# The fourth half's attention is woven in later inside the third half's feed-forward stage

## The chip, the cores and the metric

The kernel runs on one core of one Trainium2 chip. The metric is the time of one execution on the device in microseconds (us), lower is better. It is written directly against the engines: TensorE (PE) multiplies matrices into PSUM, VectorE (DVE) and ScalarE (ACT) read PSUM and write back to SBUF, GpSimd (POOL) copies and casts and issues DMAs, SyncE (SP) issues DMAs. Each engine works through its own queue in the order in which the program issued its instructions; engines meet only through semaphores.

## The reference

Windowed attention followed by a gated feed-forward network. `q`, `k`, `v` are (4, 8, 768, 64): 4 batches, 8 heads, 768 positions, head size 64.

```
scores = q @ k.T / sqrt(64) + bias          # bias = -slope[h] * distance
keep   = (key < 8) | (0 <= query - key < 96)
a      = softmax(scores where keep)         # per query
x      = (a @ v)  -> (3072 tokens, 512)     # heads side by side
out    = (relu(x @ w_gate) * (x @ w_val)) @ w_out    # d_ff = 1536
```

The output is 3072 x 512 in float32.

## The kernel before

**Halves.** The work is cut into 8 halves of 384 queries (half a batch each, `NHALF = 8`, numbered 0 to 7). Each half goes through attention, which yields `xT` (features in 4 chunks of 128, by 384 tokens), and then through the feed-forward network (FFN). The FFN of half `c` is a stage, and the attention of half `c + 1` is interleaved into that stage, piece by piece. Halves 0 and 1 have a start of their own; from half 2 on, all stages have one form. The change concerns the stage of `c = 2`, the third half, into which the attention of half 3, the fourth, is woven.

**Attention pieces** (`attention_pieces(s)`, 26 in all, for 4 pairs of heads p). `QKp.0` issues the pair's score matmuls (`pair_scores`, L397: 10 for odd halves, 8 for even ones, into 4 PSUM banks `x_ps`) and two exponentials on ACT (L406); `QKp.1` two more exponentials and the masks of the first group on DVE (L359, three for odd halves); `QKp.2` the masks of the second group (two). `AVp.0` and `AVp.1` (L427, five matmuls each) multiply by the values into one `x_ps` bank each; ACT takes the logarithm of the row sums (`lnd`, L436) and, after the second, the exponential of its negative (`rcp`, L441). `Np` (`piece_norm`, L446, two DVE products) writes the pair's chunk of `xT`. Two pieces are empty gaps. No attention piece issues a DMA.

**FFN pieces** (`ffn_pieces(c)`). `gate(fc)` does four matmuls (L518, one for each chunk of `xT`) into a bank `ff_ps`, and ACT's relu (L525) into `grelu`. `val(fc)` does the same with the other weights, and DVE multiplies by `grelu` into `ht` (L531). There are 12 pairs of gate and val. Behind some vals DVE adds columns of `ht` (`sum_de`, `sum_cb`, `sum_ad`, L567 to L576). Then come one output block of four parts (L538) and seven products `p4 p3 p1 p2 p5 p6 p7` (L583), whose results ACT and DVE collect and SP stores.

**The start of a stage.** The last chunk of `xT[c]` (chunk 3, from N3 of the stage before) comes late, so a stage begins with `begin`: the matmuls of gate 0 and val 0 on chunks 0 to 2, and for `c = 2` those of gate 1 as well. The piece `g0` is then only the matmul on chunk 3 plus the relu; likewise `v0`, and for `c = 2` also `g1`.

**Banks.** PSUM holds 3 `ff_ps` banks and 5 `x_ps` banks, each handed out in rotation. In the order g0, v0, g1, v1, g2, ... a bank comes round after three: val 1 needs the bank that gate 0's relu empties, gate 2 the one that DVE's product of val 0 empties, and in general val n+1 waits for relu n and gate n+2 for `ht` n. The scores, AVs and the products p2 and p5 take `x_ps` banks: scores 0 takes banks 0 to 3, scores 1 takes 4, 0, 1, 2, AV0 takes 3 and 4, scores 2 takes 0 to 3 (so its last bank is the one that N0 has to empty), and so on.

**The order.** Each engine's queue follows the program. `weave` issues the FFN pieces in order, each with a weight; a placed piece is issued as soon as its position, as a share of the total weight, has been passed. `spread(items, first, last)` places n items evenly from `first` to `last`.

```
def spread(items, first, last):
    n = len(items)
    return [(first + (i + 0.5) / n * (last - first), f) for i, (_, f) in enumerate(items)]

def weave(f_items, *placed):
    ...
    for t, f in f_items:
        f()
        done += t
        while ai < len(a_items) and a_items[ai][0] * total <= done:
            a_items[ai][1]()
            ai += 1
```

For `c = 2` the weights are 1.5 for `begin`, 0.15 for each of g0, v0 and g1, and 0.65 for every other piece (the three sums at the end weigh nothing): 22.75 in total. The loop is

```
    for c in range(2, NHALF):
        placed = []
        if c + 1 < NHALF:
            placed.append(spread(attention_pieces(c + 1), *((0.02, 0.8) if c == 2 else (0.0, 0.8))))
        if c + 2 < NHALF:
            load_qk(c + 2, 0, H)
            load_v_half(c + 2)
            placed.append(spread(early_pieces(c + 2), 0.25, 0.75))
        f1, f2 = ffn_pieces(c)
        weave(f1 + f2, *placed)
```

`load_qk` (SP) and `load_v_half` (POOL) fetch the half after the next; `early_pieces` are its casts (POOL), transposes (SP's DMA queue) and key copies (POOL for every half but 2).

Of the kernel before, what the change touches and what calls it, by code (L numbers as in the profile page):

```python
# [15 lines left out]
def kernel(  # L16
# [90 lines left out]
    def load_qk(s, h0, h1):  # L107
        b, half = divmod(s, 2)
        if s not in qs_of:
            qs_of[s] = late["stage"].tile([128, H, NN * D], FP32, name="qs")  # L110
            ks_of[s] = late["stage"].tile([128, H, NN * D], FP32, name="ks")
        for src, dst in ((k, ks_of[s]), (q, qs_of[s])):
            nc.sync.dma_start(
                out=dst[:, h0:h1, :],
                in_=src[b, h0:h1, half * QH : (half + 1) * QH, :].rearrange(
                    "h (p n) d -> p h (n d)", n=NN))
# [28 lines left out]
    def load_v_half(s):  # L145
        b, half = divmod(s, 2)
        if half == 0:
            load_v_globals(b)
            if s != 2:
                spread_v_globals(b)  # L150
        for j in range(4) if half == 0 else range(4, NT):
            load_v(b, j)
# [224 lines left out]
    def early_pieces(s):  # L377
        out = [(0.0, lambda p=p, i=i: piece_cast(s, p, i)) for i in range(2) for p in range(HP)]
        out += [(0.0, lambda n=n: piece_x(s, n)) for n in range(NN)]
        out += [(0.0, lambda p=p: piece_order(s, p)) for p in range(HP)]  # L380
        return out
# [26 lines left out]
    def piece_qk(s, p, g):  # L408
        if g == 0:
            pair_scores(s, p)  # L410
        if g < 2:
            pair_exps(s, p, g)
        if g > 0:
            masks(s, p, g - 1, steps_later)

    def piece_av(s, p, e):
        b, half = divmod(s, 2)
        h = 2 * p + e
        vb = vbuf[b % 2]
        av = psum["x"].tile([128, 512], FP32, name="x_ps")  # L420
        av_of[s, p, e] = av
        av3 = av[:, 0:QH].rearrange("d (n p) -> d n p", n=NN)
        todo = [by[half, j] for g in steps_later[half] for j in g]
        for i, (j, a, w, m) in enumerate(todo):
            es, c = es_of[s, p, j]
            z0 = 2 * D * h + (D if e == 0 else 0)
            nc.tensor.matmul(av3[:, :, a : a + w],  # L427
                             lhsT=vb[:, j, z0 : z0 + 128],
                             rhs=es[:, e, c : c + NN * w].rearrange("k (n p) -> k n p", n=NN),
                             start=(i == 0), stop=(i == len(todo) - 1),  # L430
                             skip_group_check=True)
        o0, d0 = (0, 64) if e == 0 else (64, 0)
        if e == 0:
            av_of[s, p, "l"] = rc_pool.tile([128, QH], FP32, name="lnd")
        ln = av_of[s, p, "l"]
        nc.scalar.activation(ln[o0 : o0 + 64], av[d0 : d0 + 64, 0:QH], AF.Ln, bias=0.0, scale=1.0)  # L436
        if e == 1:
            if s not in xT_of:
                xT_of[s] = xt_pool.tile([128, N_DC, QH], BF16, name="xT")
            rc = av_of[s, p, "r"] = rc_pool.tile([128, QH], FP32, name="rcp")  # L440
            nc.scalar.activation(rc, ln, AF.Exp, bias=0.0, scale=-1.0)  # L441

    def piece_norm(s, p):
        for e in range(2):
            r = slice(64 * e, 64 * e + 64)
            nc.vector.tensor_tensor(xT_of[s][r, p, :], av_of[s, p, e][r, 0:QH], av_of[s, p, "r"][r],  # L446
                                    op=ALU.mult)
# [45 lines left out]
    def attention_pieces(s):  # L493
        QK = lambda p: [(0.15, lambda g=g: piece_qk(s, p, g)) for g in range(3)]
        AV = lambda p: [(0.29, lambda e=e: piece_av(s, p, e)) for e in range(2)]
        N = lambda p: [(0.0, lambda: piece_norm(s, p))]
        g = QK(3)
        a = AV(2)
        gap = [(0.0, lambda: None)]
        return (QK(0) + QK(1) + AV(0) + N(0) + gap + QK(2) + AV(1) + N(1) + gap  # L500
                + g[0:1] + a[0:1] + g[1:2] + a[1:2] + g[2:3] + N(2) + AV(3) + N(3))
# [157 lines left out]
# [6 lines that stand above are left out]
        total = sum(t for t, _ in f_items)  # L665
        a_items = sorted((x for p in placed for x in p), key=lambda x: x[0])
        done, ai = 0.0, 0
# [6 lines that stand above are left out]
        for _, f in a_items[ai:]:  # L674
            f()
# [158 lines left out]
    for c in range(2, NHALF):  # L834
        placed = []
        if c + 1 < NHALF:
            placed.append(spread(attention_pieces(c + 1), *((0.02, 0.8) if c == 2 else (0.0, 0.8))))
        if c + 2 < NHALF:
            load_qk(c + 2, 0, H)
            load_v_half(c + 2)  # L840
# [3 lines that stand above are left out]
# [35 lines left out]
```

## Time and profile before

| what | us |
|---|---|
| median of 3 runs | 242.94 (242.49 to 243.86) |
| the profiled execution | 242.59 |
| its span, first to last instruction | 240.8 |
| PE busy | 233.0 (97 per cent) |
| DVE busy | 172.4 (72 per cent) |
| ACT busy | 153.4 (64 per cent) |
| POOL busy | 86.8 (36 per cent) |
| mean granted TensorE clock | 1.000 |

Times in the profile run from the span's first instruction. A line of the timeline gives the start, the duration, the engine, the line of the kernel, the operation, what it writes and reads with shapes, and how often; in square brackets stands how long the engine had been idle before it and what released it. Consecutive like instructions are merged into one line. The duration of merged matmuls includes the drain of the last one, so that the next matmul's start can lie before that end; starts are what to compare on PE. The stage of `c = 2` runs from 76.71 (the first matmul of `begin`) to 105.81 (the first of the next stage's).

### The profile page before, as it was taken

To read this page: it belongs to the slowest core of one execution; us is meant where nothing else is said; L and a number is where in the kernel's file an instruction comes from. 1 tells how busy PE (TensorE), PEld (TensorE's weight loads), DVE (VectorE), ACT (ScalarE), POOL (GpSimd) and SP (SyncE) were. 2 spreads that over 40 slices of the span, in tenths; PEclk is the share of its full clock that TensorE was granted. 3 is DMA by queue.
4 is the path that set the end of the run, shared out by engine and by line. 5 is a ranking of instruction groups with operands and counts; after the bars stand their busy time and mean duration, and the time that the engine had idled before them with its cause. 6 is when DMAs were issued, how large, how long until landed. Compare 5 with 4: busy or idle time off the path is not lost.

```text
span 240.8 us, 5354 instructions
## 1 busy us (share of the span) xinstructions
PE 233.0 (97%) x1937; PEld 146.3 (61%) x1945; DVE 172.4 (72%) x456; ACT 153.4 (64%) x347; POOL 86.8 (36%) x202
## 2 busy tenths in 40 slices
PE   7899999999999799999999999999999999999994
PEld 3655556665458456676658566676658566676663
DVE  7875965769577597866787679766888677764643
ACT  5897873438775777738864677738874677734330
POOL 6776893208514853603365041721514000000000
PEclk9999999999999999999999999999999999999999
DMA  6999999994976995748429945199251200030003
GB/s 203 187 197 177 258 233 219 180 153 81 268 159 158 295 148 109 48 136 261 89 46 110 256 131 108 25 174 268 44 95 44 87 3 0 3 123 9 4 24 107
DMA packets 69603, 31.42 MB, mean 130 GB/s; under 512 B 47160, under 2 KB 66616, under 8 KB 69576
## 3 DMA queue, kind: packets, MB, share of 16 engines
q0 software_dynamic: 31744, 8.71, 35.2%
q1 hardware_dynamic: 36616, 21.45, 34.7%
q10 hardware_dynamic: 1216, 0.92, 1.2%
q8 instruction: 15, 0.25, 0.4%
q14 instruction: 12, 0.10, 0.1%
HBM read 28.41 MB, written 6.29 MB: 144 GB/s over the span
## 4 chain that ended last, share of the span: by engine, by line
PE 92%; ACT 3%; DVE 3%; issue 1%; DVEq 0%
PE ff_ps L518 52%; PE ff_ps L538 10%; PE ff_ps L583 10%; PE x_ps L427 6%; PE x_ps L397 4%; PE x_ps L583 4%; PE t_ps L459 2%; PE s_ps L341 1%; PE t_ps L682 1%; PE t_ps L310 1%; PE t_ps L272 1%; ACT ef L347 1%; ACT es L406 1%; DVE es L359 1%; DVE xT L446 0%
## 5 line engine op out<-in xcount | busy, mean ns | idle before, releaser
L518 PE MATMUL ff_ps<-xT,wv 128*128 128x384 bf16 x384 | 80.2, 326 | 1.3 <-ACT grelu L525 1.2
L518 PE MATMUL ff_ps<-xT,wg 128*128 128x384 bf16 x384 | 80.7, 326 | 0.7 <-ACT grelu L525 0.4
L531 DVE TENSOR_TENSOR ht<-ff_ps,grelu 128x384 bf16<-128x384 f32 x96 | 53.0, 554 | 28.7 <-PE ff_ps L518 15.1
L525 ACT ACTIVATE grelu<-ff_ps 128x384 bf16<-128x384 f32 x96 | 47.2, 493 | 37.2 <-PE ff_ps L518 18.7
L518 PEld LDWEIGHTS <-wv 128*128 128x128 bf16 x384 | 36.1, 97 | 24.2 <-issue 2.5
L518 PEld LDWEIGHTS <-wg 128*128 128x128 bf16 x384 | 35.9, 98 | 24.5 <-issue 1.3
L406 ACT ACTIVATE es<-x_ps 128x360 bf16<-128x360 f32 (+2 forms) x96 | 36.6, 443 | 20.1 <-PE x_ps L397 20.0
L359 DVE TENSOR_TENSOR es<-es,m_all 128x432 bf16<-128x432 bf16 (+4 forms) x108 | 30.5, 327 | 9.6 <-ACT es L406 9.2
L446 DVE TENSOR_TENSOR xT<-x_ps,rcp 64x384 bf16<-64x384 f32 x48 | 26.6, 554 | 8.9 <-ACT rcp L441 8.2
L436 ACT ACTIVATE lnd<-x_ps 64x384 f32<-64x384 f32 x48 | 23.3, 485 | 12.3 <-PE x_ps L427 11.6
L538 PE MATMUL ff_ps<-wo_sb,ht 128*128 128x512 bf16 x112 | 29.7, 379 | 0.4
L363 POOL CAST kqc<-ks 128x384 bf16<-128x384 f32 x24 | 11.5, 525 | 34.7 <-DMA ks<-in_k_dram 34.7
L137 POOL DMA_DIRECT2D vbuf<-in_v_dram x25 | 21.6, 875 | 1.7 <-DMA wv<-in_moe_w_val_dram 1.5
L427 PE MATMUL x_ps<-es,vbuf 128*128 128x216 bf16 (+4 forms) x216 | 21.5, 225 | 0.0
L427 PEld LDWEIGHTS <-vbuf 128*128 128x128 bf16 x216 | 15.8, 97 | 7.7
L538 PEld LDWEIGHTS <-ht 128*128 128x128 bf16 x120 | 10.9, 97 | 9.4
L263 POOL COPY kT<-kqT 128x240 bf16<-128x240 bf16 x16 | 6.8, 423 | 24.6 <-DMA kqT<-kqc 21.9
L363 POOL CAST kqc<-qs 128x384 bf16<-128x384 f32 x24 | 11.9, 535 | 8.0 <-DMA qs<-in_q_dram 8.0
L259 POOL COPY kT<-kqT 128x360 bf16<-128x360 bf16 x10 | 6.2, 616 | 19.5 <-DMA kqT<-kqc 19.5
L441 ACT ACTIVATE rcp<-lnd 128x384 f32<-128x384 f32 x24 | 12.6, 524 | 0.8
L347 ACT ACTIVATE ef<-s_ps 128x720 bf16<-128x720 f32 (+2 forms) x16 | 10.9, 711 | 2.0 <-PE s_ps L341 1.8
L397 PE MATMUL x_ps<-kqT,kT 64*128 64x216 bf16 (+4 forms) x216 | 11.6, 224 | 0.2
(115 smaller groups left out, 252.7 us busy)
## 6 DMA issues: line engine op xcount, KB each, us to landing
out_dram<-osb SPq DMA_DIRECT2D x22, 256.0 KB, 2.5
ks<-in_k_dram SPq DMA_DIRECT2D x6, 768.0 KB, 5.8
qs<-in_q_dram SPq DMA_DIRECT2D x6, 768.0 KB, 11.7
vbuf<-in_v_dram POOLq DMA_DIRECT2D x21, 120.0 KB, 7.9
wg<-in_moe_w_gate_dram POOLq DMA_DIRECT2D x3, 512.0 KB, 8.3
wv<-in_moe_w_val_dram POOLq DMA_DIRECT2D x3, 512.0 KB, 9.9
wo_sb<-in_moe_w_out_dram POOLq DMA_DIRECT2D x1, 1536.0 KB, 19.9
kq<-in_q_dram ACTq DMA_DIRECT2D x2, 192.0 KB, 4.2
```

The source lines that it names most:

```text
L137: nc.gpsimd.dma_start(out=v_dst(b, NG + r0, NG + r0 + n, j), in_=v[b, :, KT * j + r0 : KT * j + r0 + n, :].rearrange("h p d -> p h d"))
L359: nc.vector.tensor_mul(for_all, for_all, mk)
L363: nc.gpsimd.tensor_copy(kqc[:, :, i].rearrange("t n (h d) -> t h n d", d=D)[:, 2 * p : 2 * p + 2], of[s][:, 2 * p : 2 * p + 2, :].rearrang ...
L406: nc.scalar.activation(es[:, e, 0:c], banks[e][:, 0:c], AF.Exp, bias=0.0, scale=scale)
L427: nc.tensor.matmul(av3[:, :, a : a + w], lhsT=vb[:, j, z0 : z0 + 128], rhs=es[:, e, c : c + NN * w].rearrange("k (n p) -> k n p", n=NN), s ...
L436: nc.scalar.activation(ln[o0 : o0 + 64], av[d0 : d0 + 64, 0:QH], AF.Ln, bias=0.0, scale=1.0)
L446: nc.vector.tensor_tensor(xT_of[s][r, p, :], av_of[s, p, e][r, 0:QH], av_of[s, p, "r"][r], op=ALU.mult)
L518: nc.tensor.matmul(st[key][:, 0:QH], lhsT=w_of(w, dc, fc), rhs=xT_of[c][:, dc, :], start=(dc == 0), stop=(dc == N_DC - 1))
L525: nc.scalar.activation(gr, psg[:, 0:QH], AF.Relu, bias=0.0, scale=1.0)
L531: nc.vector.tensor_tensor(ht[:, fc, :], psv[:, 0:QH], st["gr", fc], op=ALU.mult)
L538: nc.tensor.matmul(ps2, lhsT=ht[:, fc, n * 128 : (n + 1) * 128], rhs=wo_sb[:, fc, :], start=(fc == 0), stop=(fc == N_FC - 1))
L583: nc.tensor.matmul(st[key][:, 0:D2], lhsT=left(i), rhs=right(i), start=start and i == 0, stop=stop and i == N2 - 1, skip_group_check=not s ...
```

## The change

```
     for c in range(2, NHALF):
         placed = []
         if c + 1 < NHALF:
-            placed.append(spread(attention_pieces(c + 1), *((0.02, 0.8) if c == 2 else (0.0, 0.8))))
+            placed.append(spread(attention_pieces(c + 1), *((0.07, 0.82) if c == 2 else (0.0, 0.8))))
```

In the stage of `c = 2` alone, the 26 attention pieces of half 3 are placed from 7 to 82 per cent of the stage instead of 2 to 80. No instruction is added or removed; the order of issue changes. The other stages keep their order.

More of the change, by code (lines that the diff above doesn't have):

```diff
@@ L836 @@
         if c + 1 < NHALF:
-            placed.append(spread(attention_pieces(c + 1), *((0.02, 0.8) if c == 2 else (0.0, 0.8))))
+            placed.append(spread(attention_pieces(c + 1), *((0.07, 0.82) if c == 2 else (0.0, 0.8))))
         if c + 2 < NHALF:
```

## The prediction

> **What bounds the kernel now.** I read the chain that ended last first: 92 per cent of it is PE. PE works through one queue, so what the change can win is PE's idle time in the stage that it touches. Next I read busy time by stage, one window for each of the stages of c = 2, 3 and 4:
>
> ```profile
> core 0: us, PE busy (x) PEld busy (x) DVE busy (x) ACT busy (x) POOL busy (x), PEclk, DMA share, GB/s
> 76.70:105.80 29.10, 27.56 (x231) 17.84 (x231) 22.60 (x57) 18.90 (x44) 16.15 (x35) 1.00 0.91 141
> 105.80:132.70 26.90, 26.85 (x215) 17.45 (x215) 19.93 (x51) 18.34 (x44) 11.35 (x25) 1.00 0.70 134
> 132.70:160.20 27.50, 27.42 (x232) 17.86 (x232) 21.45 (x55) 18.98 (x44) 10.30 (x23) 1.00 0.62 129
> ```
>
> The stages of c = 2 and c = 4 have the same PE work (odd halves' attention in both, the same matmuls), yet c = 2 takes 29.10 us and c = 4 takes 27.50. The stage has 1.6 us that its twin does not need, at the same granted clock of 1.00. PE's timeline shows where:
>
> ```profile
> 77.69 0.65 PE L518 MATMUL ff_ps<-xT,wg 128*128 128x384 bf16 x3
> 78.27 0.48 PE L397 MATMUL x_ps<-kqT,kT 64*128 64x216 bf16 x10
> 78.68 0.34 PE L518 MATMUL ff_ps<-xT,wg 128*128 128x384 bf16 x1
> 78.86 0.33 PE L518 MATMUL ff_ps<-xT,wv 128*128 128x384 bf16 x1
> 79.02 0.33 PE L518 MATMUL ff_ps<-xT,wg 128*128 128x384 bf16 x1
> 80.58 0.81 PE L518 MATMUL ff_ps<-xT,wv 128*128 128x384 bf16 x4 [1.24 <-ACT grelu L525]
> 81.23 0.81 PE L518 MATMUL ff_ps<-xT,wg 128*128 128x384 bf16 x4
> ...
> 85.61 0.81 PE L518 MATMUL ff_ps<-xT,wv 128*128 128x384 bf16 x4
> 86.67 0.81 PE L518 MATMUL ff_ps<-xT,wg 128*128 128x384 bf16 x4 [0.25 <-DVE ht L531]
> ```
>
> A group of four FFN matmuls follows the next after 0.65 us (80.58 to 81.23), so one takes 0.163. The matmul at 79.02 frees PE at 79.18, and val 1 starts at 80.58: 1.40 us lost, waiting for gate 0's relu, since val 1 takes gate 0's bank. Val 4 at 85.61 frees PE at 86.26, and gate 5 starts at 86.67: 0.41 lost, waiting for DVE's product `ht` 3. ACT and DVE show why both came late:
>
> ```profile
> 78.63 1.52 ACT L406 ACTIVATE es<-x_ps 128x336 bf16<-128x336 f32 x4 [3.17 <-PE x_ps L397]
> 80.00 0.91 ACT L525 ACTIVATE grelu<-ff_ps 128x384 bf16<-128x384 f32 x2
> ```
>
> ```profile
> 77.26 1.13 DVE L446 TENSOR_TENSOR xT<-x_ps,rcp 64x384 bf16<-64x384 f32 x2
> ...
> 84.40 1.76 DVE L359 TENSOR_TENSOR es<-es,m_all 128x432 bf16<-128x432 bf16 x5
> 86.08 1.01 DVE L531 TENSOR_TENSOR ht<-ff_ps,grelu 128x384 bf16<-128x384 f32 x2
> ```
>
> ACT has four exponentials of scores 0 in front of relu 0, 78.63 to 80.15, though relu 0's matmul began at 78.68 and had drained by 79.02. DVE has both mask groups of pair 1, five masks in 1.76 us, in front of `ht` 3.
>
> **What the order becomes.** The weights sum to 22.75. Before, the pieces stand every 0.78/26 x 22.75 = 0.68, the first at (0.02 + 0.015) x 22.75 = 0.80; `begin` passes 1.5, so QK0.0 (0.80) and QK0.1 (1.48) follow it at once. After, they stand every 0.66, the first at (0.07 + 0.0144) x 22.75 = 1.92; `begin`, g0, v0 and g1 pass 1.5, 1.65, 1.8 and 1.95, so QK0.0 follows g1 and QK0.1 (2.58) follows v1 (2.6). Worked on in this way the orders are:
>
> before: begin QK0.0 QK0.1 g0 v0 g1 v1 QK0.2 g2 QK1.0 v2 QK1.1 g3 QK1.2 v3 AV0.0 g4 AV0.1 v4 N0 g5 v5 QK2.0 ... o0 N2 o1 AV3.0 o2 AV3.1 o3 N3 p4
>
> after: begin g0 v0 g1 QK0.0 v1 QK0.1 g2 QK0.2 v2 QK1.0 g3 QK1.1 v3 g4 QK1.2 v4 AV0.0 g5 AV0.1 v5 N0 g6 v6 QK2.0 ... o0 QK3.2 o1 N2 o2 AV3.0 o3 AV3.1 p4 N3
>
> So relus 0 and 1 are ahead of all exponentials, and only one mask group stands ahead of each `ht` (QK1.1 before `ht` 3, QK1.2 behind it). POOL's and SP's queues hold no attention instruction of this half, so their order is as before.
>
> **Cost, stall by stall.** (1) Val 1's wait. Chunk 3 of `xT` is ready when DVE ends at 77.26 + 1.13 = 78.39. `begin` ends at 76.71 + 9 x 0.163 = 78.18. Before, scores 0 filled that gap; now g0 waits for chunk 3. Relu 0 ended at about 80.50 and released val 1 at 80.58, so a release takes some 0.08: g0 starts at 78.47, a new stall of 0.29 (0.21 if the release is immediate, and not below that, since the norm's place on DVE does not move). Then v0 at 78.63, g1 at 78.80. Relu 0 starts when g0 has drained (0.33) at 78.84 and ends 0.49 later at 79.33, val 1 may start at 79.41. Scores 0 (0.09 of switch, seen as 81.88 to 81.97, and 0.41 of work) fill PE from 78.96 to 79.46. So val 1 starts at 79.46 without waiting: the 1.40 goes and 0.29 comes.
>
> (2) Gate 5's wait. From 79.46 on I laid the three queues side by side with the durations of the rows (relu 0.49, four exponentials 1.52, mask groups 0.65 and 0.60, `ht` 0.56, AV 0.31, `lnd` 0.49, `rcp` 0.52). `ht` 0 79.40 to 79.95, before gate 2 at 80.12; `ht` 1 to 80.88, before gate 3 at 81.93; the exponentials of pair 0 79.68 to 81.20, relu 2 81.15 to 81.64, before val 3 at 82.58; masks of pair 0 to 82.05, `ht` 2 to 82.55, before gate 4 at 83.23; masks QK1.1 to about 83.65, `ht` 3 to 84.20, before gate 5 at 84.84. Of the 0.41 nothing is left by this; if these masks go at the pace of the five (1.76 for what takes 1.25 elsewhere), `ht` 3 ends at 84.5, still in time.
>
> (3) What is late next. N0 now stands behind v5 and its sum: `ht` 5 from 86.65 to 87.21, the sum to 87.60, N0's first product to 88.17, release 88.25. It empties the bank that the eighth matmul of scores 2 takes. Scores 2 starts at 87.84, its eighth matmul at 88.13: a stall of 0.1. Before, N0's first product ended at 87.63 and scores 2 started at 88.07, no wait. The bounds are nothing (DVE 0.1 quicker) and 0.5 (DVE late by the 0.51 that the five masks lost); I take 0.1. `ht` 6 then ends at 89.30 for gate 8 at 89.66, `ht` 9, behind N1, at 94.45 for gate 11 at 95.0: covers of 0.36 and 0.5.
>
> (4) The end of the stage. AV3.1 moves behind o3, N3 behind p4, so `lnd` and `rcp` of pair 3 stand behind the block's copy on ACT; N3 ends about 102.3. Behind N3 on DVE stand the last sum, which p7 needs at 103.7, and p2's result at about 102.6. Chunk 3 is wanted by the next stage's g0 some 1.4 us after it starts near 104.4. Cost nothing; were N3 3 us later, the next stage would stall.
>
> The sum: the stage had stalls of 1.40 + 0.41 = 1.81; it now has 0.29 + 0.1 = 0.39, a gain of 1.42. Against the twin: 29.10 - 1.42 = 27.68, still 0.18 over c = 4, as the 0.29 and 0.1 against c = 4's own pauses lead one to expect. The later stages follow unchanged: their loads hang on their own stage's stores, and equal stages agree (c = 3 and c = 5 both 26.90, c = 4 and c = 6 both 27.50). The profiled execution was 242.59 and would be 241.2; the median of the three runs is 0.35 higher, which would give 241.5. I take 241.4 between them. With the bounds (0.21 at best; 0.29 + 0.5 + the whole 0.41 at worst) the gain lies between 1.6 and 0.6.
>
> **A rule against it.** The Trainium skill, in Perfetto Trace Analysis, section Matmuls, wants independent matmul groups to rotate through different PSUM banks, so that one's evacuation is overlapped by the next one's matmuls. By that rule alone the place of scores 0 before is right, for it is independent work in other banks exactly where PE waits for chunk 3, and taking it away would cost the 0.29 and make 242.9 of the profiled 242.59. The trace has the larger number on the other side: the same scores bring 1.52 us of exponentials in front of the relu that empties the bank.
>
> **The rivals.** *Half of it comes back* (no change that can be told): the norm's wait of 0.29 stays, gate 5's 0.41 stays because DVE falls behind once more, and scores 2 waits 0.3 for N0. The gain is 1.81 - 0.29 - 0.41 - 0.3 = 0.8, so 241.8 to 242.1. For it: DVE is the second busiest in this stage (22.60 of 29.10) and POOL's casts fall in the same stretch, where five masks took 1.76. Against it: `ht` 3 has 0.3 to 0.6 of cover. *The norms become the stall* (slower): N0, N1 and N2 each stand between PE and a bank of scores or an `ht` product, and each waits on ACT's `rcp`. If ACT's queue delays `rcp` and so each norm holds PE for over 0.47, three of them take the 1.42 back; at 0.9 each, 2.7, the kernel ends at 243.9. Against: N0 to N2 held PE not at all before (no such release on PE between 87 and 101), and each is moved by one FFN piece only. *The change does not do what it says*: the positions above leave no room for that, the margin (1.92 against 1.8 and 1.95 at g1) is arithmetic.
>
> **How the numbers follow.** 0.5 per cent, 1.2 us, is about what a measurement of this kernel can tell from no change. The forecast's centre of 1.42 lies just above it, so part of its own range (0.9 to 1.6) falls within. I give the forecast 0.72, the first rival 0.18, the second 0.10. Of the forecast's 0.72, some 0.60 lie beyond 0.5 per cent and 0.12 within, to which the first rival's 0.18 is added: faster 0.60, same 0.30, slower 0.10. The likeliest case's own range is 240.9 to 242.0. The range goes to 242.6 to take in the first rival and leaves out the second and a little at the low end.
>
> **What would show it.** In the changed profile, the stage from `begin` to the next `begin` should last 27.7 us. PE's timeline should show a gap of 0.3 released by DVE's `xT` ahead of g0 and none ahead of val 1; ACT should show two relus from about 78.8 and the exponentials behind them; gate 5 should follow val 4 and AV0.0 with no gap. The prediction is wrong if val 1 still waits for a relu, if PE shows new waits on DVE of over 0.5 us in total between 82 and 98, or if a later stage grows.

## The result and the profile after

The changed kernel takes 241.63 us (median of 6 runs, 241.15 to 242.14) against 242.94 us before: a ratio of 0.9939, 95 per cent interval 0.9917 to 0.9961, so 1.3 us or 0.6 per cent faster. Run again beside the experiments it took 241.75 us, ratio 0.9948 (0.9930 to 0.9965). The prediction was 241.4 us (range 240.9 to 242.6), with 0.6 on faster by over 0.5 per cent.

The busy time by stage, for the stages of c = 2 and c = 3 (the windows lie 0.1 to 0.2 us ahead of the stages' bounds, which are given below; us in the stretch, then the busy time of each engine with its instructions, the granted clock, the DMA share and GB/s):

```profile
core 0: us, PE busy (x) PEld busy (x) DVE busy (x) ACT busy (x) POOL busy (x), PEclk, DMA share, GB/s
76.70:104.50 27.80, 27.66 (x232) 17.99 (x231) 22.87 (x58) 18.88 (x44) 16.31 (x37) 1.00 0.92 146
104.50:131.40 26.90, 26.85 (x215) 17.45 (x214) 20.12 (x52) 18.34 (x44) 11.28 (x25) 1.00 0.71 134
```

From the first matmul of `begin` (76.89) to the next stage's (104.61) the stage now takes 27.72 us instead of 29.10, at the same clock. PE's timeline of the changed kernel, in the same columns as before:

```profile
77.87 1.06 PE L518 MATMUL ff_ps<-xT,wg 128*128 128x384 bf16 x4
78.77 0.32 PE L518 MATMUL ff_ps<-xT,wv 128*128 128x384 bf16 x1
78.93 0.33 PE L518 MATMUL ff_ps<-xT,wg 128*128 128x384 bf16 x1
79.19 0.48 PE L397 MATMUL x_ps<-kqT,kT 64*128 64x216 bf16 x10
79.60 0.82 PE L518 MATMUL ff_ps<-xT,wv 128*128 128x384 bf16 x4
80.26 0.81 PE L518 MATMUL ff_ps<-xT,wg 128*128 128x384 bf16 x4
...
84.02 0.81 PE L518 MATMUL ff_ps<-xT,wv 128*128 128x384 bf16 x4
84.67 0.47 PE L427 MATMUL x_ps<-es,vbuf 128*128 128x216 bf16 x5
84.98 0.81 PE L518 MATMUL ff_ps<-xT,wg 128*128 128x384 bf16 x4
...
87.98 0.67 PE L397 MATMUL x_ps<-kqT,kT 64*128 64x216 bf16 x10
88.58 0.82 PE L518 MATMUL ff_ps<-xT,wg 128*128 128x384 bf16 x4
```

Val 1 (79.60) follows scores 0 after their 0.41, gate 5 (84.98) follows AV0.0 after its 0.31: both waits are gone. Two short ones show: three matmuls of gate 1 and g0 are merged in the first line, and 1.06 where three in a row take 0.65 says that g0 stood apart; `begin` ends at 76.89 + 9 x 0.163 = 78.36, and v0 at 78.77 puts g0 at 78.61, so it waited 0.25. Scores 2 take 0.60 to the next start (87.98 to 88.58) instead of 0.41. On ACT the two relus are first:

```profile
78.96 0.87 ACT L525 ACTIVATE grelu<-ff_ps 128x384 bf16<-128x384 f32 x2 [3.33 <-PE ff_ps L518]
79.72 1.53 ACT L406 ACTIVATE es<-x_ps 128x336 bf16<-128x336 f32 x4
```

and on DVE `ht` 3 (83.64) stands between the two mask groups of pair 1, and N0 (87.72) behind `ht` 5 and its sum:

```profile
77.44 1.11 DVE L446 TENSOR_TENSOR xT<-x_ps,rcp 64x384 bf16<-64x384 f32 x2
...
82.92 0.64 DVE L359 TENSOR_TENSOR es<-es,m_all 128x432 bf16<-128x432 bf16 x3
83.64 0.56 DVE L531 TENSOR_TENSOR ht<-ff_ps,grelu 128x384 bf16<-128x384 f32 x1
84.17 1.26 DVE L359 TENSOR_TENSOR es<-es,m_all 128x384 bf16<-128x384 bf16 x2
...
87.72 1.14 DVE L446 TENSOR_TENSOR xT<-x_ps,rcp 64x384 bf16<-64x384 f32 x2
```

Of the 1.38 us that the stage won, the profiled execution (241.74 us, span 239.9) shows 0.9 at its end. The stage began 0.18 later than before, and the stages of c = 4 and c = 5 took 27.67 and 27.02 where they had taken 27.47 and 26.91: 0.31 of the gain was lost there.

### The profile page after: what moved, and what is told of

Its sections match the earlier page's. It is cut to its first block, busy times and chain, and to the rows that moved or that the text cites. A ratio compares the mean times of both kernels' runs of the same rounds, so it can differ in the third digit from the quotient of the medians.

```text
span 239.9 us, 5355 instructions
## 1 busy us (share of the span) xinstructions
PE 233.5 (97%) x1937; PEld 146.6 (61%) x1945; DVE 173.3 (72%) x456; ACT 153.4 (64%) x347; POOL 85.9 (36%) x202
## 4 chain that ended last, share of the span: by engine, by line
PE 91%; ACT 3%; DVE 2%; issue 1%; ACTq 0%
PE ff_ps L518 53%; PE ff_ps L538 9%; PE ff_ps L583 8%; PE x_ps L427 6%; PE x_ps L397 4%; PE x_ps L583 3%; PE t_ps L459 2%; PE s_ps L341 2%; PE t_ps L272 1%; PE t_ps L682 1%; ACT lnd L436 1%; PE t_ps L310 1%; DVE xT L446 1%; PE s_ps L321 1%; ACT rcp L441 0%
## 5 line engine op out<-in xcount | busy, mean ns | idle before, releaser
L359 DVE TENSOR_TENSOR es<-es,m_all 128x432 bf16<-128x432 bf16 (+4 forms) x108 | 31.2, 334 | 8.2 <-ACT es L406 7.8
```

The costliest lines, as they stand in the source:

```text
L359: nc.vector.tensor_mul(for_all, for_all, mk)
```

## The experiments

Two theories stood against each other. The queue theory is that of the prediction: the gain is the order on ACT ahead of relu 0 and on DVE ahead of `ht` 3. The rival: the attention as a whole lies later, and whatever crowding there was is eased. All results together; "stage" is the time from the first matmul of `begin` to that of the next stage in the one profiled execution of each kernel, "begin" where that first matmul lies. A ratio is taken against executions of the kernel before that were run beside that kernel.

| kernel | begin | stage | median us | ratio to before (95 per cent) |
|---|---|---|---|---|
| before | 76.71 | 29.10 | 242.94 | |
| the change | 76.89 | 27.72 | 241.63 | 0.9939 (0.9917 to 0.9961) |
| the change again | 76.81 | 27.72 | 241.75 | 0.9948 (0.9930 to 0.9965) |
| 1 exponentials first | 76.59 | 28.87 | 242.41 | 0.9976 (0.9962 to 0.9991) |
| 2 one mask group later | 77.26 | 29.11 | 242.39 | 0.9979 (0.9957 to 1.0001) |
| 3 scores first | 77.87 | 28.58 | 242.21 | 0.9972 (0.9955 to 0.9989) |
| 4 two exponentials ahead | 76.69 | 28.35 | 242.07 | 0.9963 (0.9946 to 0.9979) |
| 5 later still | 76.75 | 29.01 | 242.72 | 0.9992 (0.9977 to 1.0006) |
| 6 casts held back | 76.71 | 28.82 | 242.49 | 0.9976 (0.9959 to 0.9992) |
| 7 sum behind the norm | 76.22 | 27.53 | 240.76 | 0.9913 (0.9890 to 0.9936) |
| 8 both waits covered | 76.32 | 27.29 | 241.21 | 0.9925 (0.9898 to 0.9953) |
| 9 all even stages | 76.61 | 27.28 | 240.75 | 0.9912 (0.9888 to 0.9937) |
| 10 norm 3 sooner | 77.38 | 27.29 | 241.02 | 0.9923 (0.9905 to 0.9941) |

The column "begin" spreads over 1.65 us. The kernel before, the change and experiments 1 to 6 issue the same instructions in the same order up to `begin`, yet they range from 76.59 to 77.87; experiments 8 to 10, equal among themselves up to there, range from 76.32 to 77.38. So the stage tells the theories apart better than the time does; the change's stage came out at 27.72 both times.

**1. Exponentials first.** On the changed kernel, in the stage of c = 2, QK0.0 and QK0.1 go directly behind `begin`:

```
+               for i in range(2):
+                   items[i] = (0.05, items[i][1])
```

> The changed kernel, with one thing undone: QK0.0 and QK0.1 (the score matmuls of pair 0, its four exponentials and the masks behind them) stand directly behind begin again, as before; the other 24 attention pieces stay at their places of the change. Queue theory (the gain is ACT's order at the start, plus DVE's mask order ahead of ht 3): val 1 waits for relu 0 again, about 1.2 to 1.4 us on PE, no wait of gate 5; stage of c = 2 about 28.7 us, time about 0.4 us under before. Rival (the gain comes from the attention as a whole lying later, less crowding of DVE and ACT): 24 of 26 pieces lie where the change puts them, so nearly all of the gain stays, over 1.0 us under before.

Val 1 waits again, from 79.06 to 80.46:

```profile
80.46 0.81 PE L518 MATMUL ff_ps<-xT,wv 128*128 128x384 bf16 x4 [1.24 <-ACT grelu L525]
```

Gate 5 doesn't wait. The stage is 28.87, 0.17 over the expected 28.7: the expectation left out the wait of 0.19 in scores 2 (88.83 to 89.43, 0.60 as in the change). With 24 of 26 pieces where the change has them, 0.23 of the stage's 1.38 is left, and 0.24 of 0.6 per cent in the time. The rival, nearly all of the gain, falls.

**2. One mask group later.** On the kernel before, QK1.2 and AV0.0 change places:

```
+               items[5:7] = [(items[6][0], f) for _, f in (items[6], items[5])]
```

> The kernel before, with one piece moved: QK1.2 (two masks on DVE, nothing on ACT or PE) stands behind AV0.0, so behind ht 3 on DVE, instead of ahead of it. Queue theory: val 1 waits 1.4 us for relu 0 as before, gate 5 no longer waits for ht 3 (0.41 gone); stage about 28.7 us, time about 0.4 us under before. Rival (whole attention later): no change, 29.1 us, for 25 of 26 pieces lie as before; or the 0.41 comes back at a later gate as a wait for ht 4 or 5.

Gate 5 no longer waits: it starts 9.54 us behind `begin` (86.80) instead of 9.96. But the 0.41 comes back at scores 2:

```profile
88.20 0.40 PE L397 MATMUL x_ps<-kqT,kT 64*128 64x216 bf16 x7
88.78 0.33 PE L397 MATMUL x_ps<-kqT,kT 64*128 64x192 bf16 x3 [0.18 <-DVE xT L446]
89.04 0.82 PE L518 MATMUL ff_ps<-xT,wg 128*128 128x384 bf16 x4
```

The eighth matmul waits for N0; gate 6 starts 11.78 us behind `begin`, before it was 11.77. The stage is as long as before (29.11); the time, 0.9979 with an interval that just holds 1, can't decide between that and a small gain. So the expected 28.7 failed. What happened is the second form of the rival, the wait that moves, only at N0 and not at an `ht`.

**3. Scores first.** On the kernel before, only the four exponentials (and the first masks) of pair 0 go behind g1:

```
+               items[0:2] = [(0.05, lambda: pair_scores(c + 1, 0)),
+                             (0.085, lambda: pair_exps(c + 1, 0, 0)),
+                             (0.0851, lambda: (pair_exps(c + 1, 0, 1), masks(c + 1, 0, 0, steps_later)))]
```

> The kernel before, with the four exponentials of pair 0 (and its first masks) issued behind g1; the score matmuls of pair 0 stay directly behind begin, everything else as before. Queue theory: scores 0 cover the wait for the norm, so none of 0.25 to 0.29 ahead of g0, but they no longer cover relu 0, so val 1 starts at about 79.6 on the time axis of before, a wait of 0.4 in place of 1.40; gate 5's wait of 0.4 stays or grows, as the mask order is that of before. Stage about 28.1 to 28.3 us, time 0.8 to 1.0 us under before. Rival (whole attention later): nothing of the attention but four exponentials is moved, by some 0.5 us, so under 0.3 us of gain.

```profile
80.75 0.81 PE L518 MATMUL ff_ps<-xT,wv 128*128 128x384 bf16 x4 [0.25 <-ACT grelu L525]
...
87.28 0.81 PE L518 MATMUL ff_ps<-xT,wg 128*128 128x384 bf16 x4 [0.69 <-DVE ht L531]
```

```profile
84.35 2.41 DVE L359 TENSOR_TENSOR es<-es,m_all 128x432 bf16<-128x432 bf16 x5
```

Val 1 waits 80.33 to 80.75, 0.42 as expected: relu 0's own latency, uncovered. Gate 5's wait grew to 0.85, for PE came sooner and the five masks took 2.41 us. The stage is 28.58, a little over the expected 28.1 to 28.3, by that growth. The exponentials alone give 0.98 at val 1; 0.44 of it is lost again at gate 5.

**4. Two exponentials ahead.** Start and end at 4.5 and 82 per cent:

```
-  (0.02, 0.8)
+  (0.045, 0.82)
```

> Half a dose: attention at 4.5 to 82 per cent. QK0.0 stands directly behind begin, QK0.1 behind v1, so two exponentials instead of four (before) or none (the change) are ahead of relu 0, and one mask group ahead of ht 3. Queue theory: relu 0 runs about 79.4 to 79.9 on the time axis of before, val 1 starts near 79.95, a wait of about 0.8; no wait of gate 5 and none for the norm. Stage about 28.1 us, time about 1.0 us under before, 0.4 over the change. Rival (whole attention later): start 4.5 of 2 to 7 and end 82 of 80 to 82, so about half to three quarters of the gain and no relation of val 1's wait to the number of exponentials.

```profile
79.83 0.81 PE L518 MATMUL ff_ps<-xT,wv 128*128 128x384 bf16 x4 [0.51 <-ACT grelu L525]
```

Val 1 waits from 79.15 to 79.83, 0.68 (0.8 expected). With scores 0 directly behind `begin`, the wait is thus 0.42 with no exponential ahead of the relu (experiment 3), 0.68 with two and 1.40 with four (before): the first two cost 0.26, the next two 0.72. In the change, scores 0 stand between g1 and val 1 and cover the 0.42 as well. The stage is 28.35 instead of 28.1: scores 3, at 93.23, took 0.80 to the next start instead of 0.41, a wait of 0.39 for a bank that N1 empties.

**5. Later still.** Start and end at 12 and 85 per cent:

```
-  (0.02, 0.8)
+  (0.12, 0.85)
```

> More of the same: attention at 12 to 85 per cent. Three relus are ahead of all exponentials, but scores 0 no longer stand between g1 and val 1, they stand behind gate 2. Queue theory: relu 0 is no earlier than in the change, and nothing covers it any more, so val 1 waits about 0.4 us besides the 0.25 ahead of g0; stage about 27.9 to 28.2 us, time 0.2 to 0.4 us over the change, 0.3 to 0.5 per cent under before. Rival (the later the attention the better): stage and time under those of the change.

```profile
79.36 0.81 PE L518 MATMUL ff_ps<-xT,wv 128*128 128x384 bf16 x4 [0.25 <-ACT grelu L525]
...
85.89 0.81 PE L518 MATMUL ff_ps<-xT,wg 128*128 128x384 bf16 x4 [0.78 <-DVE ht L531]
```

Val 1 waits 78.94 to 79.36, the expected 0.4. What I had not worked out is the second wait, 0.95 at gate 5: with every piece shifted by a few places, two mask groups stand in front of `ht` 3 again, now those of pair 0, on DVE:

```profile
82.96 2.40 DVE L359 TENSOR_TENSOR es<-es,m_all 128x432 bf16<-128x432 bf16 x5
85.29 0.55 DVE L531 TENSOR_TENSOR ht<-ff_ps,grelu 128x384 bf16<-128x384 f32 x1
...
91.66 1.15 DVE L359 TENSOR_TENSOR es<-es,m_all 128x432 bf16<-128x432 bf16 x5
```

Five more per cent of shift undo the change (stage 29.01 where 27.9 to 28.2 was expected, ratio 0.9992), and the next stage lost 0.25 too (27.16 instead of 26.91; its val 0 started 0.57 after its gate 0 instead of 0.33). It is not how late the attention lies that counts but which piece stands ahead of which. And the same five masks take 2.40 us at 82.96 and 1.15 at 91.66.

**6. Casts held back.** POOL's casts run from 83.10 to 85.18 in experiment 5 and from 83.31 to 85.44 before, beside the slow masks (beside all but the first 0.1 and the last 0.2 us of the five in experiment 5, and beside the first 1.0 of the 1.76 us before):

```profile
83.10 2.08 POOL L363 CAST kqc<-ks 128x384 bf16<-128x384 f32 x4 [0.68 <-DMA ks<-in_k_dram]
```

```profile
83.31 2.13 POOL L363 CAST kqc<-ks 128x384 bf16<-128x384 f32 x4 [0.85 <-DMA ks<-in_k_dram]
```

On the kernel before, in the stage of c = 2 alone:

```
+  placed.append([(0.29, lambda: nc.gpsimd.tensor_copy(late_held, xT_of[3][0:1, 0, 0:1]))])
-  placed.append(spread(early_pieces(c + 2), 0.25, 0.75))
+  placed.append(spread(early_pieces(c + 2), 0.30, 0.75))
```

> The kernel before, attention order untouched; in the stage of c = 2 POOL's casts of the half after the next are held back until N0 has written its chunk (a copy of one element of it on POOL ahead of the casts). Port theory (the five masks ahead of ht 3 are slow because POOL's casts run beside them): with POOL idle the five masks take about 1.2 us instead of 1.76, ht 3 starts near 85.5 on the time axis of before, gate 5's wait of 0.41 is gone or under 0.1; val 1's wait of 1.40 stays; stage about 28.7 us, time 0.3 to 0.4 us under before. Rival (the masks are late only because of their place in the queue and the exponentials they wait for): the five masks still take 1.7 us or more and gate 5 still waits about 0.4. The casts, transposes and key copies end some 5 us later and are still early enough for the next stage's scores at 106.9.

DVE, POOL and PE of that kernel:

```profile
84.18 1.15 DVE L359 TENSOR_TENSOR es<-es,m_all 128x432 bf16<-128x432 bf16 x5
85.25 0.55 DVE L531 TENSOR_TENSOR ht<-ff_ps,grelu 128x384 bf16<-128x384 f32 x1
```

```profile
87.82 1.97 POOL L363 CAST kqc<-ks 128x384 bf16<-128x384 f32 x4
```

```profile
85.60 0.81 PE L518 MATMUL ff_ps<-xT,wv 128*128 128x384 bf16 x4
86.25 0.81 PE L518 MATMUL ff_ps<-xT,wg 128*128 128x384 bf16 x4
```

With the attention in its old order and POOL quiet until 87.8, the masks take 1.15 us and gate 5 follows val 4 at once. So the second stall of the kernel before had two causes, and to take away either removes it: five masks in a row ahead of `ht` 3 (experiment 2), and casts beside them. The stage is 28.82, 0.28 shorter and not 0.41: the held casts now ran beside the masks of pair 2, of which the first three took 1.55 us at 89.35 instead of 0.65, and gate 8 started 0.14 late.

**The change again**, beside the next three:

> The changed kernel itself, beside the next three on one chip: 0.5 to 0.6 per cent under before, stage of c = 2 of 27.7 us, with a wait of 0.25 ahead of g0 and of 0.19 in scores 2, no others.

It was so: 27.72, with the same two waits.

**7. Sum behind the norm.** On the changed kernel, in all stages that have sums:

```
-  behind = {2: [...], 5: [lambda: sum_de(3, 6)], ...
+  behind = {2: [...], 6: [lambda: sum_de(3, 6)], ...
```

> The changed kernel, with the sum of columns 3 to 5 (sum_de, about 0.3 us on DVE) issued behind val 6 instead of val 5, so behind N0 on DVE, in all stages that have sums. Queue theory: what scores 2 waits for (0.19 us) is N0, which empties the bank that its eighth matmul takes; N0 now ends some 0.28 earlier, so the wait goes; stage of c = 2 about 27.5 us, time 0.2 under the change, which the clock of one run cannot show and the trace can. Rival (the longer scores 2 is crowding of PE's own, or a wait for ACT's exponentials): the 0.67 of scores 2 stays.

```profile
87.31 0.48 PE L397 MATMUL x_ps<-kqT,kT 64*128 64x216 bf16 x10
87.72 0.82 PE L518 MATMUL ff_ps<-xT,wg 128*128 128x384 bf16 x4
```

Scores 2 take 0.41 again and the stage 27.53: the 0.19 was N0's. The time fell by more, 0.35 points of ratio under the change run beside it. The two profiled executions differ by 1.2 us (241.73 and 240.54): 0.59 is the earlier `begin`, which the spread above covers, 0.19 this stage, and 0.42 the stages of c = 4 and c = 5, which took 27.47 and 26.91 (27.75 and 27.05 in the change). Which of it the edit brings beyond 0.19 stays open.

**8. Both waits covered.** With the edit of 7, `begin` loses gate 1 (so that all of gate 1 stands between g0 and val 1), scores 0 go directly behind `begin`, N3 of half 2 goes ahead of p7 (the lines that give `begin` and g1 their weights are left out here):

```
-           if c == 2:
-               product(wg, "g", 1, 0, N_DC - 1)
-  weave(f1_0[G[2]] + f1_1[G[2]] + f2_0 + f2_1 + [(0.0, pieces.pop()[1])],
+  weave(f1_0[G[2]] + f1_1[G[2]] + f2_0 + f2_1[:-1] + [(0.0, pieces.pop()[1])] + f2_1[-1:],
+               items[0:2] = [(0.03, lambda: pair_scores(c + 1, 0)),
+                             (items[0][0], lambda: pair_exps(c + 1, 0, 0)), items[1]]
```

> The kernel of the moved sum, and in the stage of c = 2 both waits of the start covered: begin holds only gate 0 and val 0, scores 0 stand directly behind it (they cover the norm), the exponentials of pair 0 stay where the change puts them, behind g1, and all of gate 1 (0.65 us) stands between g0 and val 1 (it covers relu 0). N3 of half 2 is issued ahead of p7, so that it ends 0.3 us earlier on DVE. Queue theory: no wait ahead of g0 nor of val 1, stage about 27.3 us, time 0.4 to 0.5 us under the change, 0.7 to 0.8 per cent under before. Rival: p7's result, now behind N3 on DVE, frees gate 1's bank late and gives 0.2 to 0.3 back as a wait of gate 1.

```profile
77.39 0.48 PE L397 MATMUL x_ps<-kqT,kT 64*128 64x216 bf16 x10
77.81 0.34 PE L518 MATMUL ff_ps<-xT,wg 128*128 128x384 bf16 x1
77.98 0.33 PE L518 MATMUL ff_ps<-xT,wv 128*128 128x384 bf16 x1
78.14 0.81 PE L518 MATMUL ff_ps<-xT,wg 128*128 128x384 bf16 x4
78.79 0.81 PE L518 MATMUL ff_ps<-xT,wv 128*128 128x384 bf16 x4
```

No wait from `begin` to val 1, and the stage is 27.29, as expected. But the next stage took 27.19 instead of 26.91, since its val 0 started 0.60 after its gate 0 instead of 0.33:

```profile
103.61 0.49 PE L518 MATMUL ff_ps<-xT,wg 128*128 128x384 bf16 x2
104.21 0.48 PE L518 MATMUL ff_ps<-xT,wv 128*128 128x384 bf16 x2
```

Val 0 takes the bank that p6's result leaves (L624, L622 in this kernel), and DVE gave that up at 104.16. In the changed kernel the same row lies just in time: it ends at 104.46 + 0.41 = 104.87 and val 0 starts at 104.94, behind N3, a sum and four results, with no idle time between them:

```profile
101.60 1.12 DVE L446 TENSOR_TENSOR xT<-x_ps,rcp 64x384 bf16<-64x384 f32 x2 [1.22 <-ACT rcp L441]
102.74 0.36 DVE L576 TENSOR_TENSOR de<-ht 128x384 bf16<-128x384 bf16 x1
103.13 0.42 DVE L611 TENSOR_TENSOR osb<-x_ps,osb 128x256 f32<-128x256 f32 x1
...
104.46 0.41 DVE L624 TENSOR_TENSOR osb<-ff_ps,osb 128x256 f32<-128x256 f32 x1
```

The shorter stage itself did not use up this room: N3 starts 3.01 us ahead of the next stage in both kernels (101.60 of 104.61, 100.60 of 103.61). What differs is the sum behind N3, which took 0.64 instead of 0.36:

```profile
101.74 0.64 DVE L574 TENSOR_TENSOR de<-ht 128x384 bf16<-128x384 bf16 x1
```

POOL's key copies, done by 99.27 in the changed kernel, ran from 99.10 to 102.62 here, beside this sum.

**9. All even stages.** The edit of 8, with the first exponentials behind v0 in the stages of c = 4 and c = 6 too:

```
-           if c == 2:
+           if c % 2 == 0:
...
-                             (items[0][0], lambda: pair_exps(c + 1, 0, 0)), items[1]]
+                             (max(0.051, items[0][0]), lambda: pair_exps(c + 1, 0, 0)),
+                             (max(0.052, items[1][0]), items[1][1])]
```

> As the kernel with both covered, and in the stages of c = 4 and c = 6 too the first two exponentials of pair 0 are issued behind v0, so behind relu 0, instead of ahead of g0. Queue theory: val 1's wait of 0.19 us in each of the two stages goes, stages of 27.5 become 27.3, time 0.4 under the kernel with both covered, 0.8 to 1.0 per cent under before. Rival: these stages' relus have no need of it, PE's pause of 0.19 there is something else and stays.

These stages took 27.34 and 27.35 instead of 27.46 to 27.47: 0.12 each, less than the 0.19 expected. The stage of c = 3 was 27.24, with a sum of 0.69 us behind N3. The time, 0.9912, can't be told from those of 7 and 8.

**10. Norm 3 sooner.** The kernel of 9, with AV3.1 and N3 one piece sooner:

```
+           if c == 2:
+               items[-2:] = [(0.765, items[-2][1]), (0.79, items[-1][1])]
```

> As the kernel with all even stages, and AV3.1 and N3 of the stage of c = 2 one piece sooner, at the order that the kernel before had at the end (AV3.1 behind o2, N3 behind o3). Queue theory: in the change N3 waits for rcp behind the block's copy on ACT, and the six results of p2 to p7 stand behind N3 on DVE without a gap; p6's result frees the bank of the next stage's val 0 with under 0.1 us to spare, and where the stage was made 0.4 shorter val 0 waited 0.2 to 0.3 for it. With N3 sooner that wait goes: the stage of c = 3 takes 26.9 us instead of 27.2, time 0.2 to 0.3 under the kernel with all even stages. Rival: the stage of c = 3 stays at 27.2, its length comes from elsewhere.

The stage of c = 3 is 26.92 again, and val 0 follows gate 0 after 0.33, although the sum behind N3 took 0.59 here too: N3, at 100.91, stands 3.76 us ahead of the next stage instead of 3.01, and that covers it:

```profile
104.67 0.49 PE L518 MATMUL ff_ps<-xT,wg 128*128 128x384 bf16 x2
105.00 0.49 PE L518 MATMUL ff_ps<-xT,wv 128*128 128x384 bf16 x2
```

From `begin` of c = 2 to that of c = 7 this kernel took 136.00 us, against 136.80 for the change and 137.86 before: the least of all. Its time, 241.02, isn't the least; in its profile `begin` lay at 77.38, later than in 7 to 9. Kernels 7 to 10 beat the kernel before by 0.75 to 0.88 per cent; 7 and 9 lie 1.0 us under the change run beside them (240.76 and 240.75 against 241.75); for 8, 0.5 us under it, the intervals overlap widely, and 10 wasn't run beside it. Among the four the runs don't decide.

## Why the prediction was right, step by step

- *Val 1's wait, 1.40 out and 0.29 in.* Measured: 1.40 out, 0.25 in. Val 1 was forecast 2.75 us behind `begin` (79.46 against 76.71) and started 2.71 behind it. Experiments 1, 3 and 4 show the cause: the wait follows the exponentials ahead of relu 0. They are 0.98 of the 1.40; the other 0.42 is relu 0's own latency, which scores 0 cover at their new place, as the prediction laid out.
- *Gate 5's wait, 0.41 out.* Measured so; gate 5 was forecast 8.13 behind `begin` and started 8.09. The prediction named the order on DVE; it saw that the five masks were slow and, in its first rival, that POOL's casts fall there, but it did not draw the one from the other (experiment 6).
- *Scores 2, 0.1 in.* The right wait at the right matmul, 0.19 instead of 0.1 (experiment 7). In experiment 2 the same wait takes back all of the 0.41, so the first rival, half of it comes back, was a real danger. `ht` 3 stands between the mask groups in both kernels; what differs is that N0 starts with scores 2 in experiment 2 (88.19 and 88.20) and 0.26 ahead of them in the change (87.72 and 87.98).
- *The end of the stage, nothing.* True in the time, wrong in the margin. I named p7's sum and the next g0 as the first to suffer, and 3 us as the room. The first is p6's result, which frees the next stage's val 0 bank, and the room is under 0.1 us. This margin was wrong, at no cost here; a sum that took 0.28 longer used it up in experiment 8, and experiment 10 made room again.
- *The later stages, unchanged.* This step failed, and by the prediction's own third sign ("or if a later stage grows") it was wrong here: both profiles of the change have a wait at AV3.0 of c = 4 (0.50 and 0.51 to the next start instead of 0.31), where two masks took 0.93 us instead of 0.60. Together with c = 5 it gave back 0.31 and 0.42 us. Why is not shown. POOL's key copies ran beside these two masks before as well (152.75 to 153.84), only shifted against them; and c = 5 took 27.01 in experiment 2 too, where the stage of c = 2 was as long as before, so its 0.1 doesn't come from a shorter stage.
- *The sum.* 1.42 forecast for the stage, 1.38 measured (1.81 less the two waits of 0.25 and 0.19 is 1.37; that the errors of the two terms, 0.04 and 0.09, have opposite signs is luck). In the time, the gain was 1.31 by the medians, 1.06 in the second comparison (242.81 against 241.75). The forecast of 241.4 was 0.2 low, or 0.35 against the second median; the later stages gave back about as much, but `begin` alone moves by more between executions. The prediction states the range of its gain twice, 0.6 to 1.6 and 0.9 to 1.6; the gains by the medians lie in both.
- *The rule on banks*, from the Trainium skill, Perfetto Trace Analysis, section Matmuls, had it right that the place of scores 0 covered a wait: 0.25 us, measured. It is half of the picture: the exponentials that the group puts on the evacuating engine's queue cost 0.98, and at its old place it left another 0.42 uncovered. Experiment 8 has both ends covered.

## What to carry to other kernels

When PE waits for a bank, look at what stands in the evacuating engine's queue ahead of the instruction that empties it, and count it: here four exponentials ahead of the relu cost 0.98 us of PE, two only 0.26. A share of a stage is a poor handle for this, since five per cent in the same direction undid the gain; order the few pieces that matter explicitly, put independent matmuls over each latency, and check the end of the stage too, where the margin here was under 0.1 us. A stall that is removed in one place can go to the next buffer in line, as 0.41 us did in experiment 2, so follow the schedule to the next two or three waits before summing.

## What the runs showed of the hardware

DVE's masks (a product of two bf16 operands, both in SBUF) slow down by about two when POOL casts beside them: the same five took 1.15 us with POOL quiet (experiment 6) and 1.76, 2.41 and 2.40 with the casts alongside (before, where they covered the first 1.0 us; experiments 3 and 5). The same holds over all 13 traces from the stage of c = 2 on: groups of three masks took 0.63 to 0.65 us with POOL neither casting nor copying, and 1.26 to 1.55 where casts ran for over nine tenths of them (six groups). The Trainium skill names such a conflict in SBUF — State Buffer, section Who interferes with whom: a DVE instruction with two SBUF inputs contends with a GpSimd instruction that reads SBUF. The runs agree, and show that it can reach PE: 0.41 us at gate 5.
